# Exponentials in PSUM, V's low part summed by the matmul, a third query/key buffer, and steps with a choice of engine

## Chip, core and metric

The kernel runs on one core of a Trainium2 chip. The metric is device time in microseconds (us); lower is better. Engines: PE (TensorE; PEld is its weight load), DVE (VectorE), ACT (ScalarE), POOL (GpSimd), SP (SyncE, which issues the DMAs).

## What is computed

Block-causal attention over 8 batches of 8 heads, 576 positions, 64 columns per head, and on its output a mixing step of rank 32 over the positions and a feed-forward network (FFN) over the channels:

```python
# per batch and head: S = 576, D = 64, blocks of 64
scores = where(block(i) >= block(j), q @ k.T / sqrt(D), -1e9)
attn = exp(scores - max(scores))
x = (attn / (sum(attn) + 1e-9)) @ v          # heads side by side: 576 x 512
u = x + (x.T @ U @ V).T                      # rank 32
out = u + relu(u @ w_ch1) @ w_ch2            # 512 -> 2048 -> 512
```

All of it is held to float32 accuracy, so a value is split into a high part that the matmul takes (float16, or float32r) and a low part, the difference; a product is then two or three matmuls.

## The kernel before, in words

**Per head.** `split_qk` (L1104) fetches q and k of a head into `raw`. ACT copies them as float32r into `qa` and `ka` (L1117, L1118), POOL subtracts to get the low parts (L1120, L1125), and three DMAs put halves together: `qb` holds q's low part over a copy of its high part, `kb` the reverse for k, where the low part reaches its partitions by a DMA from `raw` (L1136). `qa`, `ka`, `qb`, `kb` and `raw` have `NB` = 2 buffers. `maxima` (L1183) multiplies five row tiles of 128 queries by the keys that they see, DVE takes each row's maximum from PSUM (L1212), PE transposes the maxima (L1219), and DVE spreads them over five rows of `qa` (L1225), so that the next products subtract them. `probabilities` (L1232) forms the transposed scores in three groups of 640, 448 and 512 columns (two matmuls each, L1243 and L1244), ACT takes exponentials from PSUM into `p` in SBUF (L1251), ACT casts `p` to float16 `ph` (L1257), and DVE writes the low part `pl` = `p` - `ph` (L1259). `apply_v` (L1263) runs 15 pairs of matmuls: `ph` times V's high part, a column of ones and V's low part together (129 columns, L1280), and `pl` times V's high part and the ones (65 columns, L1283). The low part's result lies in columns of its own: ACT copies it out (`tmp`, L1292), DVE adds it (`sum`, L1302) and makes the inverse denominators (L1295, L1298), POOL multiplies (`x`, L1307). This runs twice per head, for two and three row tiles.

**Per pair of heads** `split_v` (L1140) scales V by a power of two and splits it; `mix` (L1314) does the rank-32 step. **Per batch** two chunks of 288 positions go through the first half of the FFN (`ffn_chunk`: L631 and L656 on PE, 12 matmuls for each of 8 hidden tiles, whose low part `hl` DVE writes at L639; the chunk's input is split at L600). These matmuls fill PE's waits once a batch's eight heads are done. The FFN's weights are split in `weights_of` (L437; low parts on DVE, L460). After attention the rest of the FFN's first half follows, with more PSUM banks (`bg`), and then its second half as block products (L873).

**Order.** At run time semaphores alone hold the engines to one another; the order of each engine's list is made before: `Plan` (L132) holds tasks with an engine, a planned duration and a priority, plays them through when the program is built, and writes each engine's list in that order. PSUM banks are given out in the same pass, four of one bank (`ba`) and one of two (`bw`). `port` keeps some DVE instructions and POOL's from being planned at one time.

```python
for g, (a, b, tiles) in enumerate(GROUPS):      # L1236
    add("PE", ..., products, [*qa.parts, ka, *qb.parts, *kb.parts], [bank])
    add("ACT", _act(b - a) + 40, pr, exponentials, [bank], [p.parts[g]])
    add("ACT", ..., lambda at=at: nc.scalar.copy(ph[:, at], p[:, at]), ...)
    add("DVE", ..., lambda at=at: nc.vector.tensor_sub(pl[:, at], p[:, at], ph[:, at]), ..., port=True)
```

Of the kernel before, what the change touches and what calls it, by code (L numbers as in the profile page):

```python
# [50 lines left out]
INTO = {"PE": 355, "DVE": 60, "ACT": 60, "POOL": 200, "SP": 60}  # L51
# [14 lines left out]
NB = 2  # L66
# [64 lines left out]

class Plan:  # L132
# [8 lines left out]
    def add(self, engine, ns, prio, fn, reads=(), writes=(), hold=(), after=0, port=False):  # L141

        n = len(self.tasks)
        ns *= 1 + 0.04 * ((n * 40503 + 7919 * VARIANT) % 65536 / 65536 - 0.5)
# [13 lines left out]
        self.tasks.append((engine, ns, prio, fn, deps, after, slots, port or engine == "POOL"))  # L158

    def issue(self, tc):  # L160
        tasks = self.tasks
        users = [[] for _ in tasks]
        left = [len(t[4]) for t in tasks]
        for n, t in enumerate(tasks):
            for d in t[4]:
                users[d].append(n)
        others = [{tasks[u][0] for u in x} for x in users]
        ready = {e: [] for e in ENGINES}
        busy = dict.fromkeys(ready, False)
        port, held, last = False, 0, None  # L170
        behind = mybir.DependencyInfo(mybir.DependencyClass.Sync, mybir.DependencyReason.DATA)
        for n, t in enumerate(tasks):
            if not left[n]:
                heapq.heappush(ready[t[0]], (t[2], n))
# [4 lines left out]
        while done < len(tasks):  # L179
            for e, q in ready.items():  # L180
# [3 lines left out]
                while q:  # L184
                    n = heapq.heappop(q)[1]
                    new = [b for b in tasks[n][6] if b.ap is None]
                    if all(b.pool for b in new) and not (port and tasks[n][7]) and not (e == "POOL" and now < held):
                        break
                    later.append((tasks[n][2], n))
                    n = None  # L190
                else:
                    n = None
# [7 lines left out]
                x = tasks[n][3]()  # L200
# [8 lines left out]
                port = port or tasks[n][7]
                end = now + tasks[n][1]  # L210
                heapq.heappush(events, (end, 0, n))
                t = end + tasks[n][5] + TAIL[e]
                heapq.heappush(events, (t + 35, 1, n))
                for x in others[n]:
                    heapq.heappush(events, (t + INTO[x], 3 + ENGINES.index(x), n))
                if not tasks[n][5]:
                    heapq.heappush(events, (end + (0 if e == "PE" else NEAR), 2, n))
            now = events[0][0]
            while events and events[0][0] <= now:
                _, kind, n, *e = heapq.heappop(events)  # L220
                if e:
                    busy[e[0]] = False
                    continue
                if kind == -1:
                    continue
                if kind == 0:
                    busy[tasks[n][0]] = False
                    port = port and not tasks[n][7]
                    continue
                if kind == 1:  # L230
                    for b in tasks[n][6]:
# [4 lines left out]
                for u in users[n]:  # L236

                    near = tasks[u][0] == tasks[n][0] and not tasks[n][5]
                    if kind == (2 if near else 3 + ENGINES.index(tasks[u][0])):
                        left[u] -= 1  # L240
                        if not left[u]:
                            heapq.heappush(ready[tasks[u][0]], (tasks[u][2], u))
# [21 lines left out]
def attention_then_mixer(  # L264
# [172 lines left out]
    def weights_of(half_bufs, hi, lo, blocks, scale, prio, limit=None):  # L437
# [15 lines left out]
        for n, b in enumerate(half_bufs["out"]):  # L453
            add(
                "ACT", _act(CW, True) + 90, last,
                lambda n=n: nc.scalar.activation(hi(n), raw[:, n, :], AF.Copy, scale=scale[:, 0:1]), [x[n], scale], [b],
            )
            add(
                "DVE", 1.3 * CW, last,
                lambda n=n: nc.vector.scalar_tensor_tensor(  # L460
                    out=lo(n), in0=raw[:, n, :], scalar=scale[:, 0:1], in1=hi(n), op0=ALU.mult, op1=ALU.subtract
                ),
                [x[n], scale, b], [b], port=True,
            )

# [214 lines left out]
    def block_products():  # L680
# [5 lines left out]
        end.writers = [n for n, t in enumerate(plan.tasks) if 0 <= t[2] < 1e6]  # L686
# [328 lines left out]
    raw_r = ring(ap, NB, [P, 2 * S], F32, "raw")  # L1015
    qa_r = [b.split(2) for b in ring(ap, NB, [P, W], F32R, "qa")]
    ka_r = ring(ap, NB, [P, W], F32R, "ka")
    qb_r = [b.split(2) for b in ring(ap, NB, [P, S], F32R, "qb")]
    kb_r = [b.split(2) for b in ring(ap, NB, [P, W], F32R, "kb")]
    p_r = [b.split(3) for b in ring(ap, 2, [P, PW], F32, "p")]  # L1020
    ph_r = [b.split(3) for b in ring(ap, 2, [P, PW + 64], F16, "ph")]
    pl_r = [b.split(3) for b in ring(ap, 2, [P, PW + 64], F16, "pl")]
    mx_r = [b.split(5) for b in ring(ap, 2, [P, P], F32, "mx")]
    vr_r = ring(ap, 2, [P, 10, D], F32, "vr")
# [3 lines left out]
    rv_r = [b.split(2) for b in ring(ap, 2, [P, 5], F32, "rv")]  # L1028
    tmp_r = ring(ap, 2, [P, 3, D], F32, "tmp")
    sum_r = ring(ap, 2, [P, 3, D], F32, "sum")  # L1030
    x_r = [b.split(4) for b in ring(ap, 2, [P, 5, P], F32, "x")]
# [8 lines left out]
    sel = buf(ap, [P, 5, P], F32, "sel")  # L1040
# [3 lines left out]
    marks = p_r[0][low, : 2 * W]  # L1044
    nc.gpsimd.memset(marks, 0.0)
    nc.gpsimd.memset(p_r[0][96:101, W : 2 * W], 1.0)
    for n, fill in enumerate((1.0, NEG)):
        x = marks[:, n * W : (n + 1) * W].rearrange("p (i h c) -> p i h c", i=5, h=2)
# [10 lines left out]
    for n in range(NB):  # L1059
        nc.vector.tensor_copy(qa_r[n][low], marks[:, 0:W])  # L1060
        nc.vector.tensor_copy(ka_r[n][low], marks[:, W : 2 * W])
        nc.vector.memset(f32(qa_r[n][0:64, 0:64]), 0.0)
        nc.vector.memset(f32(ka_r[n][0:64, S:W]), 0.0)
        nc.vector.memset(f32(kb_r[n][:, S:W]), 0.0)
# [403 lines left out]
```

## Time and profile before

| | |
|---|---|
| runs shown | 1183.0, 1181.78, 1183.11 us, median 1183.0 |
| profiled execution | 1183.07 us; its span, first to last instruction, 1181.3 us |
| mean granted TensorE clock | 0.949 of 2.4 GHz |
| busy share of the span | PE 93%, PEld 76%, DVE 84%, ACT 63%, POOL 42% |
| HBM | 76.23 MB read, 29.49 MB written |

How to read it: busy time is the union of an engine's instructions. Back-to-back instructions overlap a little at their ends, so count times mean duration is more than busy time. PE's matmuls overlap, since the pipeline's latency is in each one's duration; their cost is the step from start to start. The granted clock has two levels, 1.2 and 2.4 GHz; a mean between them is a stretch that had both.

### The profile page before, as it was taken

How to read it: one execution, taken by the hardware profiler on the slowest of the kernel's cores; microseconds unless marked ns; L12 is line 12 of the kernel's file. 1: busy time of each engine (PE TensorE's matmuls, PEld its weight loads, DVE VectorE, ACT ScalarE, POOL GpSimd, SP SyncE). 2: the span in 40 equal slices, each digit the busy share in tenths (PEclk: the TensorE clock that was granted, in tenths of full speed). 3: DMA queues.
4: the chain of work that ended last, by engine and by line, in shares of the span. 5: the costliest groups of instructions: out<-in, count | busy, mean ns of one | idle time of the engine just before them, and what ended most of it. 6: DMA issues, size and time to landing. Idle time of an engine off the chain costs nothing.

```text
span 1181.3 us, 25529 instructions
## 1 busy us (share of the span) xinstructions
PE 1095.8 (93%) x9514; PEld 903.3 (76%) x9514; DVE 991.5 (84%) x2120; ACT 747.6 (63%) x1472; POOL 491.6 (42%) x572
## 2 busy tenths in 40 slices
PE   6776897789999999999999999999999999999998
PEld 5665676677888778888888778777777777777777
DVE  7788898989898898888788785264499999999998
ACT  6566786776876887878687775424445455455543
POOL 5654444446757567565665663945400000000000
PEclk7567698979999999999999999999999999999999
DMA  5644555545545554553645432252203412431321
GB/s 135 161 111 138 135 164 161 150 113 169 159 132 151 155 140 123 137 133 92 162 102 155 112 92 61 72 161 63 86 31 111 122 41 82 121 97 40 106 81 41
DMA packets 82924, 135.71 MB, mean 115 GB/s; under 512 B 10352, under 2 KB 54384, under 8 KB 82800
## 3 DMA queue, kind: packets, MB, share of 16 engines
q1 hardware_dynamic: 82800, 134.08, 40.9%
q8 instruction: 75, 1.23, 0.4%
q14 instruction: 49, 0.40, 0.1%
HBM read 76.23 MB, written 29.49 MB: 90 GB/s over the span
## 4 chain that ended last, share of the span: by engine, by line
PE 54%; DVE 22%; ACT 15%; issue 3%; POOL 3%; DMA 2%; SPq 0%; POOLq 0%; ACTq 0%; DVEq 0%
PE bb L873 28%; PE bf L656 6%; DVE mx L1212 5%; DVE pl L1259 4%; PE bf L631 4%; ACT p L1251 4%; ACT ph L1257 3%; PE bg L631 2%; DVE qa L1225 2%; PE bg L656 2%; PE ba L1280 2%; PE ba L1243 1%; DVE hl L639 1%; DVE sum L1302 1%; PE bw L1243 1%
## 5 line engine op out<-in xcount | busy, mean ns | idle before, releaser
L1259 DVE TENSOR_TENSOR pl<-p,ph 128x448 f16<-128x448 f32 (+2 forms) x192 | 141.6, 762 | 10.3 <-ACT ph L1257 9.7
L1280 PE MATMUL ba<-vv,ph 128*128 128x129 f16 x960 | 109.0, 230 | 15.8 <-ACT p L1251 8.1
L656 PE MATMUL bf<-hh,w2h 128*128 128x288 f16 x424 | 121.9, 287 | 0.0
L656 PE MATMUL bf<-hl,w2h 128*128 128x288 f16 x424 | 121.3, 286 | 0.0
L656 PE MATMUL bf<-hh,w2l 128*128 128x288 f16 x424 | 121.3, 286 | 0.0
L631 PEld LDWEIGHTS <-w1h 128*128 128x128 f16 x1024 | 97.3, 99 | 30.0 <-issue 5.4
L656 PEld LDWEIGHTS <-w2h 128*128 128x128 f16 x1024 | 100.6, 98 | 25.5 <-issue 0.7
L873 PE MATMUL bb<-hh,w1h 128*128 128x288 f16 x448 | 118.9, 286 | 0.0
L873 PE MATMUL bb<-hh,w1l 128*128 128x288 f16 x448 | 118.9, 286 | 0.0
L873 PE MATMUL bb<-hh,w2h 128*128 128x288 f16 x448 | 118.9, 286 | 0.0
L873 PE MATMUL bb<-hh,w2l 128*128 128x288 f16 x448 | 118.9, 286 | 0.0
L1257 ACT CAST ph<-p 128x448 f16<-128x448 f32 (+2 forms) x192 | 116.1, 643 | 0.4
L1120 POOL TENSOR_TENSOR qb<-raw,qa 64x576 fp32r<-64x576 f32 x64 | 90.4, 1412 | 49.1 <-DVE pl L1259 14.8
L1283 PE MATMUL ba<-vv,pl 128*128 128x65 f16 x960 | 106.1, 201 | 5.0 <-DVE pl L1259 4.7
L1283 PEld LDWEIGHTS <-pl 128*128 128x128 f16 x960 | 89.9, 102 | 24.2 <-issue 12.2
L801 ACT CAST hh<-hb 128x576 f16<-128x576 f32 x96 | 63.8, 666 | 68.1 <-DVE hb L827 45.8
L873 PEld LDWEIGHTS <-w1h 128*128 128x128 f16 x896 | 87.7, 98 | 22.0
L873 PEld LDWEIGHTS <-w2h 128*128 128x128 f16 x896 | 87.7, 98 | 22.0
L1307 POOL TENSOR_TENSOR x<-sum,rv 128x128 f32<-128x128 f32 (+1 forms) x128 | 57.6, 457 | 105.3 <-DVE sum L1302 54.8
L1280 PEld LDWEIGHTS <-ph 128*128 128x128 f16 x960 | 92.3, 103 | 7.6 <-DVE sum L1302 2.8
L1125 POOL TENSOR_TENSOR raw<-raw,ka 64x576 f32<-64x576 f32 x64 | 90.7, 1417 | 7.8 <-issue 2.1
L873 PE MATMUL bb<-hl,w1h 128*128 128x288 f16 x448 | 91.6, 286 | 0.0
(192 smaller groups left out, 3263.0 us busy)
## 6 DMA issues: line engine op xcount, KB each, us to landing
raw<-in_qk_dram SPq DMA_DIRECT2D x63, 288.0 KB, 3.8
st<-in_w_dram SPq DMA_DIRECT2D x32, 512.0 KB, 3.8
o_d<-ot SPq DMA_DIRECT2D x72, 144.0 KB, 2.3
vr<-in_v_dram SPq DMA_DIRECT2D x32, 320.0 KB, 3.4
qb<-qa SPq DMA_DIRECT2D x64, 144.0 KB, 2.5
kb<-ka SPq DMA_DIRECT2D x64, 144.0 KB, 2.6
kb<-raw SPq DMA_DIRECT2D x64, 144.0 KB, 2.4
ur<-u_d SPq DMA_DIRECT2D x64, 144.0 KB, 2.7
```

What stands on the lines that cost most here:

```text
L631: nc.tensor.matmul(ps[:, :T], w()[wn][:, k, fs], m[k].ap, start=(i == 0), stop=(i == len(ops) - 1))
L656: nc.tensor.matmul(ps[:, :T], w()[wn][:, f, ms], hs[f][x].ap, start=(i == 0), stop=(i == len(ops) - 1))
L801: add("ACT", _act(2 * T, True), E, lambda: nc.scalar.copy(h.ap, x[0]()), [x[1]], [h])
L873: nc.tensor.matmul(bank[:, i, :T], x()[:, w(k)], p.ap[:, k, :], start=first and n == 0, stop=last and n == len(ops) - 1)
L1120: "POOL", 1380, pr, lambda: nc.gpsimd.tensor_sub(qb[top], raw[top, 0:S], f32(qa[top, 64:W])), [raw, qa.parts[0]],
L1125: lambda: nc.gpsimd.tensor_sub(raw[top, S : 2 * S], raw[top, S : 2 * S], f32(ka[top, 0:S])), [ka], [raw],
L1212: lambda i=i, view=view: nc.vector.tensor_reduce(out=mx[:, 96 + i : 97 + i], in_=view(), op=ALU.max, axis=AX.XY if i == 4 else AX.X, negat ...
L1257: add("ACT", _act(b - a, True), pr + 2, lambda at=at: nc.scalar.copy(ph[:, at], p[:, at]), [p.parts[g]], [ph.parts[g]])
L1259: "DVE", _dve(b - a), pr + 2, lambda at=at: nc.vector.tensor_sub(pl[:, at], p[:, at], ph[:, at]),
L1280: nc.tensor.matmul(bank[:, o : o + wide], ph[:, w], vv[:, 5 * s + j, 0:wide], start=(j == 0), stop=False)
L1283: nc.tensor.matmul(bank[:, o : o + D + 1], pl[:, w], vv[:, 5 * s + j, 0 : D + 1], start=False, stop=(j == i))
L1307: lambda: nc.gpsimd.tensor_tensor(out=x[:, cs, 64 * s : 64 * s + 64], in0=total[:, :n, :], in1=rv[:, cs].unsqueeze(2).to_broadcast([P, n, ...
```

## The change

- The exponential writes its result back over the scores in the PSUM bank. The cast to `ph` and the difference `pl` read the bank, which is free only after the difference. `p` is gone; the difference no longer counts as `port`.
- V's low part is multiplied by a matmul of its own (64 columns) that adds onto the high part's columns. All five row tiles share one bank; `tmp` and `sum` are gone, and DVE multiplies by the inverse denominators out of PSUM.
- `qa`, `qb` and the keys, now one tile `kk` for `ka` and `kb`, have three buffers; `raw` keeps two. k's low part is written to its partitions directly, so one of three DMAs per head goes.
- The maxima are copied out of PSUM (`mr`) and spread from there.
- A task may have several engines. Planning gives it to the first free one, unless another would end it sooner, with a handicap in ns as the last number. Such tasks: the casts and differences of q and k, V's scale, cast and difference, the copy and the spreading of maxima, two of `mix`, and the weights' cast and difference.

Short: the parts of the diff that the text speaks of.

```diff
-NB = 2
+NB = 3
...
+                    sooner = any(max(now, until.get(o, 0)) + w[0] + w[3] < now + ns + late for o, w in t.ways.items() if o != e)
+                    if not sooner and all(b.pool for b in new) and not (port and shared) and not (e == "POOL" and now < held):
...
+        add("SP", 550, pr, fetch, writes=[raw], after=DL)
+        for dst, x, b in ((qa[top, 64:W], slice(0, S), qa.parts[0]), (kk[top, 0, 0:S], slice(S, 2 * S), kk.parts[0])):
+            add(
+                "ACT", _act(S, True), pr, lambda dst=dst, x=x: nc.scalar.copy(dst, raw[:, x]), [raw], [b],
+                others=[("DVE", 64 + 0.55 * S, lambda dst=dst, x=x: nc.vector.tensor_copy(dst, raw[:, x]), True, 200)],
+            )
...
+            add(
+                "POOL", 1340, pr, sub(nc.gpsimd), [raw, a], [b], others=[("DVE", 68 + 1.042 * S, sub(nc.vector), True, 600)],
+            )
...
+        add(
+            "ACT", _act(P), pr + 2, lambda: nc.scalar.copy(mr[rows], bank[rows, 0:P]), [bank], [mr],
+            others=[("DVE", _dve(P), lambda: nc.vector.tensor_copy(mr[rows], bank[rows, 0:P]), False, 50)],
+        )
...
+        add(
+            "POOL", 1340, pr + 2, spread(nc.gpsimd), [mr], [qa.parts[1]], others=[("DVE", _dve(W), spread(nc.vector), True, 500)],
+        )
...
             add(
-                "DVE", _dve(b - a), pr + 2, lambda at=at: nc.vector.tensor_sub(pl[:, at], p[:, at], ph[:, at]),
-                [p.parts[g], ph.parts[g]], [pl.parts[g]], port=True,
-            )
+                "ACT", _act(b - a) + 90, pr,
+                lambda view=view: nc.scalar.activation(view(), view(), AF.Exp, bias=lift[:, 0:1], scale=SCALE), [], [bank],
+            )
+            add(
+                "ACT", _act(b - a), pr + 1, lambda at=at, view=view, shaped=shaped: nc.scalar.copy(shaped(ph[:, at]), view()), [bank],
+                [ph.parts[g]],
+            )
+            add(
+                "DVE", _dve(b - a), pr + 1,
+                lambda at=at, view=view, shaped=shaped: nc.vector.tensor_sub(shaped(pl[:, at]), view(), shaped(ph[:, at])),
+                [bank, ph.parts[g]], [pl.parts[g]],
+            )
...
+                        nc.tensor.matmul(bank[:, o : o + D + 1], ph[:, w], vv[:, y, 0 : D + 1], start=(j == 0), stop=False)
+                        nc.tensor.matmul(bank[:, o : o + D], ph[:, w], vv[:, y, D + 1 : 2 * D + 1], start=False, stop=False)
+                        nc.tensor.matmul(bank[:, o : o + D + 1], pl[:, w], vv[:, y, 0 : D + 1], start=False, stop=(j == i))
...
+            lambda: nc.vector.tensor_tensor(
+                out=x[:, :, 64 * s : 64 * s + 64], in0=view()[:, :, 0:D], in1=rv.ap.unsqueeze(2).to_broadcast([P, 5, D]), op=ALU.mult
             ),
```

The planner's table of choices moves the lists as follows (counts of the built programs, whole run): of 128 q/k casts DVE takes 47, of 128 q/k differences 34, of 64 spreads 19 (POOL 45), of 64 copies of maxima 27 (ACT 37), of 32 V casts 11 and differences 5; POOL scales V 14 times of 32. Behind the last matmul of `mix` PE has 888 FFN matmuls of the first half before, and 1,116 now. Ahead of the 16th `hl` on DVE, and of its matmuls on PE:

| count | before | now |
|---|---|---|
| PE: matmuls for maxima / pairs with V / probabilities | 112 / 225 / 204 | 102 / 240 / 200 |
| PE: FFN matmuls, first and second product | 192, 96 | 192, 96 |
| DVE, all | 474 | 435 |
| DVE spreads of maxima; copies `mr` | 18; 0 | 3; 6 |
| DVE row maxima | 93 | 85 |
| DVE low parts of P (`pl`) | 46 | 50 |
| DVE denominators (two instructions each) | 60 | 32 |
| DVE `sum`; scaled write of `x` | 30; 0 | 0; 16 |
| DVE weights: low part; cast | 12; 0 | 6; 2 |
| DVE q/k differences; casts; V casts; `mix` cast; `mix` difference | 0 | 4; 3; 2; 1; 1 |

PE at the start, from the first transpose of maxima (`ba`, `bw` are PSUM banks; `qa_156` and so on are buffers). Before:

```order
L1219 MATMUL ba_92<-ident,mx_170 128x128
L1243 MATMUL bw<-qa_156,ka_158 128x320
L1244 MATMUL bw<-qb_160,kb_162 128x320
L1243 MATMUL bw<-qa_156,ka_158 128x256
L1244 MATMUL bw<-qb_160,kb_162 128x256
```

Now:

```order
L1237 MATMUL ba_92<-ident,mx_169 128x128
L1237 MATMUL ba_93<-ident,mx_170 128x128
L1166 MATMUL ba_92<-ident,vm_179 128x128
L1220 MATMUL bw<-kk_161,qa_158 128x288 x2
L1222 MATMUL bw<-kk_161,qa_158 128x64
L1222 MATMUL ba_95<-kk_161,qa_158 128x448
L1266 MATMUL ba_94<-qa_156,kk_159 128x448
L1267 MATMUL ba_94<-qb_162,kk_159 128x448
```

The third head's maxima now stand ahead of the first head's products.

PE at the first product with V. Before:

```order
L1244 MATMUL ba_95<-qb_161,kb_163 128x192
L1280 LDWEIGHTS ph_166
L1280 MATMUL ba_92<-vv_174,ph_166 128x129
L1283 LDWEIGHTS pl_168
L1283 MATMUL ba_92<-vv_174,pl_168 128x65
```

Now:

```order
L1305 LDWEIGHTS ph_165
L1305 MATMUL ba_93<-vv_176,ph_165 128x65
L1306 LDWEIGHTS ph_165
L1306 MATMUL ba_93<-vv_176,ph_165 128x64
L1307 LDWEIGHTS pl_167
L1307 MATMUL ba_93<-vv_176,pl_167 128x65
```

Each pair became a triple, with a weight load for each matmul.

DVE behind the first head's product with V. Before:

```order
L1295 TENSOR_SCALAR rv_180<-ba_92,sv_178 128x2
L1298 RECIPROCAL rv_180<-rv_180 128x2
L1302 TENSOR_TENSOR sum_185<-ba_92,tmp_183 128x128
L1295 TENSOR_SCALAR rv_180<-ba_94,sv_178 128x3
L1298 RECIPROCAL rv_180<-rv_180 128x3
L1259 TENSOR_TENSOR pl_169<-p_165,ph_167 128x640
L1302 TENSOR_TENSOR sum_184<-ba_94,tmp_182 128x192
```

Now:

```order
L1288 TENSOR_TENSOR pl_168<-ba_92,ph_166 128x512
L1229 TENSOR_REDUCE mx_169<-ba_95 128x1 x2
L1312 TENSOR_SCALAR rv_182<-ba_93,sv_180 128x5
L1315 RECIPROCAL rv_182<-rv_182 128x5
L359 TENSOR_SCALAR z_99<-z_99 96x288
L1320 TENSOR_TENSOR x_184<-ba_93,rv_182 128x5x64
```

Six instructions for a head became three, and the last now writes `x` itself.

## Rows read from the trace of the kernel before

**Rows 1.** The profile's page: busy time of each engine over the span with its share and instruction count, and the span in 40 equal slices (busy tenths; PEclk is the granted TensorE clock in tenths).
```profile
PE 1095.8 (93%) x9514; PEld 903.3 (76%) x9514; DVE 991.5 (84%) x2120; ACT 747.6 (63%) x1472; POOL 491.6 (42%) x572
...
PE   6776897789999999999999999999999999999998
...
PEclk7567698979999999999999999999999999999999
```

**Rows 2.** Busy time by stretch. Columns: stretch, its length, then busy us and instruction count of PE, PEld, DVE, ACT and POOL, the granted clock, the DMA share and GB/s.
```profile
0.00:140.00 140.00, 96.15 (x575) 81.77 (x575) 116.06 (x288) 90.91 (x181) 76.28 (x93) 0.67 0.53 140
140.00:225.00 85.00, 73.92 (x663) 60.93 (x661) 77.70 (x187) 61.05 (x130) 36.47 (x43) 0.93 0.54 152
225.00:300.00 75.00, 64.22 (x591) 53.99 (x590) 67.03 (x174) 56.27 (x115) 38.45 (x51) 0.91 0.49 135
300.00:551.00 251.00, 241.56 (x2355) 204.45 (x2353) 218.75 (x546) 194.93 (x421) 159.17 (x192) 1.00 0.52 140
551.00:737.00 186.00, 179.88 (x1759) 151.98 (x1757) 144.27 (x362) 134.53 (x297) 111.51 (x136) 1.00 0.43 112
737.00:848.00 111.00, 110.06 (x893) 86.73 (x892) 46.68 (x102) 43.01 (x78) 69.74 (x58) 1.00 0.32 97
848.00:1181.30 333.30, 330.05 (x2695) 263.40 (x2692) 321.02 (x466) 166.90 (x254) 0.00 (x0) 1.00 0.26 79
```

**Rows 3.** The chain of waits in order of time (start, us, what), its last long piece.
```profile
848.77 329.29 PE bb L873 x2688
```

**Rows 4.** Timeline, all engines: where the first FFN chunk begins (start, us, engine, line, operation).
```profile
138.57 1.80 DVE L600 SCALAR_TENSOR_TENSOR ul<-ur,sc,uh 128x288 f16<-128x288 f32 x4
...
140.20 1.18 PE L631 MATMUL bf<-uh,w1h 128*128 128x288 f16 x4
```

**Rows 5.** DVE's groups by form in the stretch 0 to 225 us, which ends with the 16th hidden tile of the FFN (L639 x16). Columns: line, engine, operation, out<-in, shapes, count; busy us, mean ns of one; idle time before them and what ended it.
```profile
L1225 DVE TENSOR_TENSOR qa<-ba,sel 5x640 fp32r<-5x640 f32 x18 | 14.9, 830 | 3.1 <-PE ba L1219 2.7
L1212 DVE TENSOR_REDUCE mx<-bw 128x1 f32<-128x576 f32 x19 | 14.3, 751 | 2.0 <-PE bw L1205 1.9
L1259 DVE TENSOR_TENSOR pl<-p,ph 128x640 f16<-128x640 f32 x16 | 13.1, 821 | 2.5 <-ACT ph L1257 2.4
L344 DVE SCALAR_TENSOR_TENSOR z<-st,z 128x512 int32<-128x512 int32 x15 | 12.1, 818 | 0.0
...
L1259 DVE TENSOR_TENSOR pl<-p,ph 128x512 f16<-128x512 f32 x15 | 10.4, 694 | 0.0
L1259 DVE TENSOR_TENSOR pl<-p,ph 128x448 f16<-128x448 f32 x15 | 9.4, 630 | 0.0
...
L1212 DVE TENSOR_REDUCE mx<-ba 128x1 f32<-128x320 f32 x18 | 8.7, 483 | 0.1
...
L639 DVE SCALAR_TENSOR_TENSOR hl<-bf,hh 128x288 f16<-128x288 f32 x16 | 7.2, 452 | 2.0 <-ACT hh L636 1.9
L339 DVE TENSOR_SCALAR z<-z 128x512 int32<-128x512 int32 x15 | 6.4, 439 | 0.0
...
L460 DVE SCALAR_TENSOR_TENSOR w1l<-wr,sc,w1h 128x512 f16<-128x512 f32 x8 | 5.5, 748 | 1.5 <-ACT w1h L456 1.5
L1302 DVE TENSOR_TENSOR sum<-ba,tmp 128x192 f32<-128x192 f32 x15 | 5.1, 338 | 0.0
L1302 DVE TENSOR_TENSOR sum<-ba,tmp 128x128 f32<-128x128 f32 x15 | 4.2, 278 | 0.7 <-ACT tmp L1292 0.5
...
L1295 DVE TENSOR_SCALAR rv<-ba,sv 128x3 f32<-128x3 f32 x15 | 3.3, 218 | 5.4 <-ACT tmp L1292 3.5 <-PE ba L1283 1.8
...
L1298 DVE RECIPROCAL rv<-rv 128x3 f32<-128x3 f32 x15 | 2.7, 178 | 0.5
```

**Rows 6.** Groups by form over the whole span, all engines, same columns as rows 5.
```profile
L1120 POOL TENSOR_TENSOR qb<-raw,qa 64x576 fp32r<-64x576 f32 x64 | 90.4, 1412 | 49.1 <-DVE pl L1259 14.8 <-DVE rv L1295 7.7 <-DVE mx L1212 4.6
...
L1259 DVE TENSOR_TENSOR pl<-p,ph 128x640 f16<-128x640 f32 x64 | 56.9, 889 | 10.0 <-ACT ph L1257 9.4
...
L1251 ACT ACTIVATE p<-bw,lift 128x640 f32<-128x640 f32 x64 | 50.8, 794 | 28.6 <-PE bw L1244 23.2 <-DVE pl L1259 4.9
...
L1257 ACT CAST ph<-p 128x640 f16<-128x640 f32 x64 | 46.7, 730 | 0.1
...
L1321 POOL TENSOR_TENSOR xl<-x,xh 128x512 fp32r<-128x512 f32 x32 | 41.1, 1286 | 21.3 <-DVE pl L1259 7.3 <-ACT xh L1318 6.5 <-DVE wr L352 2.5
...
L827 DVE TENSOR_TENSOR hb<-bb,hb 128x576 f32<-128x576 f32 x32 | 24.2, 755 | 1.4 <-PE bb L873 0.7
L827 DVE TENSOR_TENSOR hb<-hb,hb 128x576 f32<-128x576 f32 x32 | 23.9, 754 | 0.0
```

**Rows 7.** PE's timeline at full clock, the product with V of one head: the first two of its 15 pairs and the last.
```profile
501.28 0.22 PE L1280 MATMUL ba<-vv,ph 128*128 128x129 f16 x1
501.33 0.19 PE L1283 MATMUL ba<-vv,pl 128*128 128x65 f16 x1
501.36 0.22 PE L1280 MATMUL ba<-vv,ph 128*128 128x129 f16 x1
...
502.49 0.22 PE L1280 MATMUL ba<-vv,ph 128*128 128x129 f16 x1
```

**Rows 8.** DMA issues by line: count, KB each, median us from issue to landing.
```profile
kb<-raw SPq DMA_DIRECT2D x64, 144.0 KB, 2.4
```

More of the change, by code (lines that the diff above doesn't have):

```diff
@@ L129, with __init__ @@
 ENGINES = ("DVE", "PE", "ACT", "POOL", "SP")
+class Task:
+    def __init__(self, ways, prio, deps, after, slots):
+        self.ways, self.prio, self.deps, self.after, self.slots = ways, prio, deps, after, slots
+        self.goal, self.near = "any" if len(ways) > 1 else next(iter(ways)), None
 class Plan:
@@ L139, in __init__, with add @@
         self.tasks = []
[L141 removed]
+    def add(self, engine, ns, prio, fn, reads=(), writes=(), hold=(), after=0, port=False, others=()):
         n = len(self.tasks)
[L144 removed]
+        k = 1 + 0.04 * ((n * 40503 + 7919 * VARIANT) % 65536 / 65536 - 0.5)
         deps = set()
@@ L157, in add @@
             b.users += 1
-        self.tasks.append((engine, ns, prio, fn, deps, after, slots, port or engine == "POOL"))
+        ways = {e: (t * k, f, p or e == "POOL", late) for e, t, f, p, late in ((engine, ns, fn, port, 0), *others)}
+        self.tasks.append(Task(ways, prio, deps, after, slots))
     def issue(self, tc):
@@ L185, in issue @@
                     n = heapq.heappop(q)[1]
-                    new = [b for b in tasks[n][6] if b.ap is None]
-                    if all(b.pool for b in new) and not (port and tasks[n][7]) and not (e == "POOL" and now < held):
+                    if taken[n]:
+                        n = None
+                        continue
+                    t = tasks[n]
+                    ns, fn, shared, late = t.ways[e]
+                    new = [b for b in t.slots if b.ap is None]
+                    sooner = any(max(now, until.get(o, 0)) + w[0] + w[3] < now + ns + late for o, w in t.ways.items() if o != e)
+                    if not sooner and all(b.pool for b in new) and not (port and shared) and not (e == "POOL" and now < held):
                         break
-                    later.append((tasks[n][2], n))
+                    later.append((t.prio, n))
                     n = None
@@ L199, in issue @@
                 done += 1
-                x = tasks[n][3]()
+                taken[n] = True
+                t.near = None if t.after else e
+                x = fn()
                 if e == "POOL" and last is not None:
@@ L203, in issue @@
                     last = None
-                if e == "DVE" and tasks[n][7]:
+                if e == "DVE" and shared:
                     last = x
-                    held = now + tasks[n][1] + PORT
+                    held = now + ns + PORT
                     heapq.heappush(events, (held, -1, n))
                 busy[e] = True
[L209 to L217, printed above, removed]
+                port = port or shared
+                end = until[e] = now + ns
+                heapq.heappush(events, (end, 0, n, e, shared))
+                at = end + t.after + TAIL[e]
+                heapq.heappush(events, (at + 35, 1, n))
+                for x in goals[n]:
+                    heapq.heappush(events, (at + INTO[x], 3, n, x))
+                if not t.after:
+                    heapq.heappush(events, (end + (0 if e == "PE" else NEAR), 2, n, e))
             now = events[0][0]
@@ L236, in issue @@
                 for u in users[n]:
-                    near = tasks[u][0] == tasks[n][0] and not tasks[n][5]
-                    if kind == (2 if near else 3 + ENGINES.index(tasks[u][0])):
+                    if tasks[u].goal == e[0] and (kind == 2) == (e[0] == tasks[n].near):
                         left[u] -= 1
                         if not left[u]:
-                            heapq.heappush(ready[tasks[u][0]], (tasks[u][2], u))
+                            arrive(u)
+        self.end = now
 def _act(n, sbuf=False):
@@ L1140, in split_v @@
+        for dst, y, a, b in ((qb[low], qa[top, 64:W], qa.parts[0], qb.parts[1]), (kk[top, 1, 0:S], kk[top, 0, 0:S], kk.parts[0], kk.parts[1])):
+            add("SP", 530, pr, lambda dst=dst, y=y: nc.sync.dma_start(out=f32(dst), in_=f32(y)), [a], [b], after=DL)
     def split_v(p, pr):
```

226 lines of the change are left out of this document (94 added, 132 removed).

## The prediction

> **What bounds the kernel now.** I read the page first: PE is busy for 93% of the span, and its slices show where it is not, the first ten, in which PEclk falls as well [rows 1]. Then the stretches [rows 2]. From 0 to 140 us PE's busy time is 96 of 140 us at a mean granted clock of 0.67, so between the two levels, and most often at 1.2 GHz; DVE is busy for 116. From 140 to 225 us DVE has 78 of 85, its fullest stretch of the attention stage. From 300 us to 737 us, where the last matmul of attention stands, PE is busy for 421 of 437 us at full clock, and DVE for 363. Then comes FFN work alone, and from 848 us a block stage of 2,688 matmuls in 329.3 us, 122.5 ns each [rows 3]; the change touches nothing there. The first FFN chunk could not start before 138.6 us, when its scaled input was split [rows 4]; until then PE has nothing to fill its waits with.
>
> So the time is PE's work plus what PE loses, and it loses most before 225 us, where DVE's list sets the pace: ahead of the 16th hidden tile DVE's 474 instructions keep it busy for 193.8 of 225 us [rows 2, 5]. Two places decide: when the FFN starts to fill PE, and when attention ends with how much FFN work left.
>
> **The start, up to the 16th hidden tile.** The counts stand in the table of the change. PE has issued nearly the same there (192 and 96 FFN matmuls in both; ten fewer matmuls for maxima, 15 more pairs of V). DVE's list differs, each count priced by its row [rows 5]:
> - spreading the maxima: 18 to 3 of 0.830: -12.4 us; six copies of 128 columns in its place, priced by the 128-column sum, 0.278: +1.7.
> - sums of V's two parts: 15 x 0.338 + 15 x 0.278 = 9.2 go; 16 scaled writes of 320 columns come, 0.338 plus twice the 0.060 that 64 columns cost: 0.458, in all 7.3: -1.9.
> - denominators: 60 instructions, about 0.214 and 0.172 (11.6) become 32 on five columns, some 0.436 a head (7.0): -4.6.
> - eight fewer maxima at 0.483, the middle size: -3.9.
> - the low part of P: 46 to 50. It now reads PSUM. The maxima read PSUM too and cost 0.483 at 320 columns and 0.751 at 576, so 0.818 at 640 and 0.707 in the mean of the three sizes, against 0.715 (0.821, 0.694, 0.630): 35.4 against 32.9: +2.5. That PSUM itself costs DVE nothing is in two rows, 755 ns from PSUM and 754 from SBUF for 576 columns [rows 6].
> - low parts of weights: 12 of 0.748 become six differences of about 0.69 and two casts of about 0.44 (priced by L339): -4.0.
> - work that DVE takes over by the planner's choice: four q/k differences of 0.754, three q/k casts of 0.48, two V casts of 0.53, one of each for the mixing (0.44, 0.69): +6.6.
> - one more step each of the four that split a weight block, 0.44 to 0.82: +2.5.
>
> The sum is -13.5, and I take all of it as time, because DVE paces this stretch and PE's own work in it is the same. A cast could cost as much as a difference (0.75), which takes 2 us off; if the waits between engines shrink with the list, as 193.8 of 225 does, it is 16.
>
> **V's low part.** A pair now takes 1.21 us / 14 = 86 ns, 129 columns some 55 and 65 columns some 30, each with its own weight load [rows 7]. The third matmul of 64 or 65 columns should cost what the 65 do: 3 x 30 = 90, so +3.6 ns x 960 pairs, less the 225 pairs ahead of the 16th hidden tile, where PE isn't full: +2.6 us. Bounds: 81 ns if only the columns count, -4 us; three times today's mean of 43 ns, 129, +31 us. I take the first price since its row is the same instruction.
>
> The Trainium skill, TensorE: Matmul & The Clock Gate, section Back-to-back issue gap, speaks against this part: a stream of weight load and matmul pairs sustains some 81 ns per matmul at 128 columns. By it a pair would be 162 ns now and 243 afterwards, 960 x 81 = 78 us more, and the sum 1248; the trace has 86 for two, so the measurement decides.
>
> **What else is moved, and what covers it.** ACT loses 128 copies of V's low part, 47 q/k casts and more, and gains 37 copies of maxima. Its exponentials now write PSUM; no row shows that. The nearest is 0.794 us into SBUF for 640 columns [rows 6]. I take no change, with -0.05 and +0.1 each as ends: 192 x 0.1 = 19 us on an engine idle for 107 of 437 us from 300 to 737 [rows 2], so at nothing. If that cover were gone, the cast behind it and P's low part would be late. The Trainium skill, ScalarE: Activation LUTs, section Step-by-step: what each stage is for, calls PSUM the lower-latency destination; no run here shows it yet, and by it this term could only fall.
>
> A PSUM bank is now held until DVE has taken P's low part. The widest bank serves 1,920 columns of maxima and products (0.9 us at 30 ns for 65 [rows 7]), two reductions (1.0 [rows 5]), exponential 0.8, cast 0.7, difference 0.8: 4.2 us, some 5.5 with the hops, where a head comes every 11.5 (737 us / 64). So it is covered, but PE's maxima for the next head queue behind it. Spreading on POOL waits for a copy on ACT or DVE and takes longer than DVE's 0.83; POOL's nearest row, 1.286 for 512 columns, gives 1.5 for 640. That is 1 us more in a head's chain, 45 times; with a third buffer another head's products lie beside it, and without them 17 early heads would cost up to 17 us. Against it stand V's shorter end (one write where there were a copy, a sum and a POOL product) and 64 DMAs of 2.4 us that no longer stand between a difference and its products [rows 8], each one issue less on SP. I set these against each other at nothing. POOL loses 128 products and some differences.
>
> **The sum.** The profiled execution took 1183.07 us, 0.07 above the median of the runs: 1183.1 - 13.5 + 2.6 = 1172.2; I say 1172.
>
> **The other account, and the rivals.** In the new order attention ends with 1,116 FFN matmuls to go, not 888. That is 228 x 122.5 ns = 27.9 us more behind it, so attention must end 27.9 + 2.6 us sooner, at 707 us, to break even, and at 695 for my number. By the prices above DVE's list to the end of attention changes by: spreads -37.4, copies +7.6, sums -10.1, denominators -21.5, P's low part -11 (0.889 over the run to 0.818, and so for the others [rows 5, 6]), weights -4.6, work taken over +68, fewer FFN tiles -7: -16. So DVE's 623.8 busy us [rows 2] become 608, and 695 means that DVE is 87.5% busy.
>
> - **DVE paces all of attention (slower, 0.26).** DVE keeps its share over the stage, 623.8 / 737 = 85%: attention ends at 718, and the time is 1183 + 27.9 + 2.6 - 19 = 1195. The point that decides is a share of 86%. For it: the work that DVE takes over eats most of its savings. Against it: the share was 87% up to 551 us and fell to 78% after, where PE was 97% busy and DVE waited for PE.
> - **Choice closes DVE's gaps (0.20).** With two engines for a step and P's low part out of POOL's way (14.8 us of POOL's idle time ahead of L1120 ended with L1259, and that instruction grew from 0.821 early to 0.889 overall [rows 5, 6]) DVE reaches 90%: attention ends at 675, and 1183 + 27.9 + 2.6 - 61 = 1152. The Trainium skill, SBUF — State Buffer, section Who interferes with whom, says that a DVE instruction with two SBUF inputs contends with GpSimd's reads and one with at most one doesn't; by it P's 192 differences leave the contest and some 115 casts and differences of DVE enter it.
> - **The early gain is given back (0.08).** The FFN starts sooner but waits for batch 1's heads as before: 1183, no change.
> - **V is bound by its loads (0.03).** At 129 ns a pair, where PE is full, the end moves by +31 - 13.5: 1201.
>
> **How the numbers follow.** My forecast, 1160 to 1180 us by the two ends named for the start and V's lower bounds, has 0.43. The range reaches to both larger rivals with 2 or 3 us for their shares: 1149 to 1196; V's loads and the far ends of those two stay outside. A change under 0.2%, 2.4 us, can't be told from none. Faster: 0.43 + 0.20 = 0.63; same 0.08; slower 0.26 + 0.03 = 0.29.
>
> **What would show it.** The 16th hidden tile near 212 us; the first split of FFN input near 125; attention's last matmul at about 695 with DVE 87% busy up to there; V's three steps about 30 ns each at full clock; the exponentials within 0.1 us of their old times; PE over 95% busy from 300 us on. I am wrong if attention ends after 707, if PE's products wait for banks by more than 0.3 us a head, or if V's triple takes over 110 ns.

## The result, and the profile after

The changed kernel takes 1142.9 us (median of four runs, 1140.5 to 1144.0) against 1183.05 (1181.8 to 1185.2) for the kernel before: ratio 0.966, 95% interval 0.9635 to 0.9677, 40 us faster. The forecast was 1172, 11 us faster.

The page: PE's share rose from 93 to 95%, DVE's from 84 to 86%, ACT's and POOL's fell [rows 1]. PE's low slices end earlier.

```profile
PE 1081.7 (95%) x10474; PEld 894.8 (78%) x10474; DVE 986.0 (86%) x2025; ACT 683.9 (60%) x1315; POOL 463.6 (41%) x461
...
PE   5767888899999999999999999999999999999998
...
PEclk6778898799999999999999999999999999999999
```

Stretches, in the columns of [rows 2]: up to the first FFN matmul (120.2 us; 140.2 before [rows 4]), up to the 16th hidden tile's low part (201.6; before 225), the full-clock middle, the whole of attention, and what follows.

```profile
0.00:120.20 120.20, 84.56 (x760) 72.46 (x761) 105.28 (x256) 82.58 (x165) 80.50 (x82) 0.75 0.51 139
0.00:201.60 201.60, 157.00 (x1495) 131.44 (x1496) 182.45 (x435) 143.68 (x291) 128.34 (x126) 0.83 0.56 153
300.00:551.00 251.00, 246.70 (x2846) 210.67 (x2845) 241.28 (x573) 180.54 (x380) 146.20 (x147) 1.00 0.47 128
0.00:670.70 670.70, 614.13 (x6664) 522.41 (x6665) 611.83 (x1444) 467.66 (x969) 389.27 (x395) 0.94 0.48 131
670.70:809.00 138.30, 138.30 (x1126) 109.56 (x1125) 53.95 (x118) 49.23 (x94) 74.30 (x66) 1.00 0.30 87
809.00:1141.60 332.60, 329.31 (x2689) 262.81 (x2686) 320.27 (x465) 167.03 (x254) 0.00 (x0) 1.00 0.26 79
```

Attention's last matmul of `mix` stands at 670.3 us instead of 737, with DVE busy for 91% up to there. The chain's last long piece begins 39.7 us earlier and is as long as before [rows 3], so the whole gain lies ahead of it:

```profile
809.03 329.29 PE bb L892 x2688
```

Groups by form, in the columns of [rows 5] and [rows 6]:

```profile
L1246 POOL TENSOR_TENSOR qa<-mr,sel 5x640 fp32r<-5x640 f32 x45 | 69.8, 1553 | 34.1 <-ACT mr L1241 8.1 <-DVE qa L1246 6.6 <-DVE vm L1158 4.3
L1142 POOL TENSOR_TENSOR qb<-raw,qa 64x576 fp32r<-64x576 f32 x48 | 69.1, 1439 | 51.8 <-ACT qa L1135 8.8 <-PE bf L675 6.6 <-issue 5.7
...
L1288 DVE TENSOR_TENSOR pl<-bw,ph 128x640 f16<-128x640 f32 x64 | 52.1, 813 | 6.5 <-ACT ph L1283 6.1
L1280 ACT ACTIVATE bw<-bw,lift 128x640 f32<-128x640 f32 x64 | 49.2, 768 | 43.0 <-PE bw L1267 39.9 <-DVE z L359 1.5 <-DVE rv L1315 1.0
...
L1283 ACT CAST ph<-bw 128x640 f16<-128x640 f32 x64 | 44.7, 699 | 0.8 <-PE ba L1307 0.4
...
L1320 DVE TENSOR_TENSOR x<-ba,rv 128x320 f32<-128x320 f32 x64 | 30.9, 484 | 0.5
...
L1312 DVE TENSOR_SCALAR rv<-ba,sv 128x5 f32<-128x5 f32 x64 | 13.9, 217 | 11.8 <-PE ba L1307 11.6
L1142 DVE TENSOR_TENSOR qb<-raw,qa 64x576 fp32r<-64x576 f32 x16 | 13.4, 835 | 0.0
L1315 DVE RECIPROCAL rv<-rv 128x5 f32<-128x5 f32 x64 | 12.2, 191 | 2.2
```

V's triples at full clock, the first and the twelfth of a run on PE:

```profile
500.08 0.19 PE L1305 MATMUL ba<-vv,ph 128*128 128x65 f16 x1
500.11 0.20 PE L1306 MATMUL ba<-vv,ph 128*128 128x64 f16 x1
500.14 0.19 PE L1307 MATMUL ba<-vv,pl 128*128 128x65 f16 x1
...
501.09 0.19 PE L1305 MATMUL ba<-vv,ph 128*128 128x65 f16 x1
```

Eleven steps in 1.01 us: 92 ns a triple, 31 ns a matmul.

### The profile page after: what moved, and what is told of

Its sections match the earlier page's. It is cut to its first block, busy times and chain, and to the rows that moved or that the text cites. A ratio compares the mean times of both kernels' runs of the same rounds, so it can differ in the third digit from the quotient of the medians.

```text
span 1141.6 us, 27034 instructions
## 1 busy us (share of the span) xinstructions
PE 1081.7 (95%) x10474; PEld 894.8 (78%) x10474; DVE 986.0 (86%) x2025; ACT 683.9 (60%) x1315; POOL 463.6 (41%) x461
## 4 chain that ended last, share of the span: by engine, by line
PE 67%; DVE 21%; ACT 4%; issue 3%; DMA 2%; POOL 2%; SPq 0%; DVEq 0%; POOLq 0%; ACTq 0%
PE bb L892 29%; PE bf L675 8%; PE bf L650 8%; DVE mx L1229 5%; PE bg L675 4%; DVE pl L1288 4%; PE bg L650 3%; PE ba L1305 2%; PE ba L1306 2%; PE ba L1307 2%; PE ba L1266 1%; PE bw L1266 1%; PE bw L1267 1%; DVE hl L658 1%; PE ba L1267 1%
## 5 line engine op out<-in xcount | busy, mean ns | idle before, releaser
L675 PE MATMUL bf<-hh,w2h 128*128 128x288 f16 x384 | 110.6, 288 | 1.4 <-DVE hl L658 1.4
L675 PE MATMUL bf<-hh,w2l 128*128 128x288 f16 x384 | 109.9, 286 | 0.0
L675 PE MATMUL bf<-hl,w2h 128*128 128x288 f16 x384 | 109.8, 286 | 0.0
L1305 PE MATMUL ba<-vv,ph 128*128 128x65 f16 x960 | 108.4, 199 | 0.9 <-DVE pl L1288 0.6
L1306 PE MATMUL ba<-vv,ph 128*128 128x64 f16 x960 | 107.6, 200 | 0.0
L1305 PEld LDWEIGHTS <-ph 128*128 128x128 f16 x960 | 92.7, 100 | 5.3 <-issue 3.0
L1306 PEld LDWEIGHTS <-ph 128*128 128x128 f16 x960 | 93.5, 101 | 1.9 <-issue 1.0
L1307 PEld LDWEIGHTS <-pl 128*128 128x128 f16 x960 | 93.6, 103 | 0.1
L892 PE MATMUL bb<-hl,w2h 128*128 128x288 f16 x448 | 91.5, 286 | 0.0
L1280 ACT ACTIVATE ba<-ba,lift 128x448 f32<-128x448 f32 (+1 forms) x128 | 79.0, 630 | 19.2 <-PE ba L1267 18.8
L1142 POOL TENSOR_TENSOR qb<-raw,qa 64x576 fp32r<-64x576 f32 x48 | 69.1, 1439 | 51.8 <-ACT qa L1135 8.8
```

Source lines behind the costliest of these rows:

```text
L675: nc.tensor.matmul(ps[:, :T], w()[wn][:, f, ms], hs[f][x].ap, start=(i == 0), stop=(i == len(ops) - 1))
L892: nc.tensor.matmul(bank[:, i, :T], x()[:, w(k)], p.ap[:, k, :], start=first and n == 0, stop=last and n == len(ops) - 1)
L1142: sub = lambda e, dst=dst, x=x, y=y: lambda: e.tensor_sub(dst, raw[:, x], f32(y))
L1280: lambda view=view: nc.scalar.activation(view(), view(), AF.Exp, bias=lift[:, 0:1], scale=SCALE), [], [bank],
L1305: nc.tensor.matmul(bank[:, o : o + D + 1], ph[:, w], vv[:, y, 0 : D + 1], start=(j == 0), stop=False)
L1306: nc.tensor.matmul(bank[:, o : o + D], ph[:, w], vv[:, y, D + 1 : 2 * D + 1], start=False, stop=False)
```

## One account for all runs

PE's work is nearly the same in all these kernels, so they are compared by **PE's loss**: a stretch less its matmuls, each priced by its columns at full clock (288 take 122.5 ns [rows 3], others in proportion; floors of 29 ns, and of 58 or 110 for narrow float32 ones, estimates from the shortest steps in the traces). Time at half clock counts as loss. The level of a loss hangs on these floors; its differences between runs move by 1 or 2 us with other floors. Stretches: to the first FFN matmul ("start"), to 250 us, to attention's last matmul of `mix`, and the block stage. The time is the median of a kernel's runs; the losses are those of its profiled execution.

| run | us | first FFN | start | to 250 | to end | block | end of attention |
|---|---|---|---|---|---|---|---|
| before | 1183 | 140 | 88 | 36 | 37 | 0 | 737 |
| before, other orders (e7, e8) | 1179, 1180 | 135, 138 | 84, 85 | 35, 36 | 39, 36 | 0 | 718, 733 |
| changed | 1143 | 120 | 68 | 31 | 21 | 0 | 670 |
| changed, other orders (e5, e6) | 1158, 1149 | 127, 120 | 71, 70 | 39, 29 | 24, 26 | 0 | 658, 644 |
| changed, fixed engines (e1) | 1165 | 129 | 80 | 34 | 28 | 0 | 696 |
| changed, two buffers (e2) | 1199 | 123 | 74 | 30 | 25 | 45 | 759 |
| changed, exponentials in SBUF (e3) | 1179 | 125 | 75 | 43 | 37 | 0 | 659 |
| changed, V's old form (e4) | 1175 | 125 | 68 | 40 | 44 | 0 | 666 |
| before + exponentials in PSUM (e9) | 1161 | 121 | 72 | 34 | 32 | 0 | 702 |
| the same, `pl` kept as `port` (e16) | 1171 | 142 | 89 | 30 | 25 | 6 | 743 |
| before + V in PSUM (e10) | 1155 | 131 | 79 | 33 | 20 | 3 | 718 |
| the same + DVE load (e14) | 1159 | 127 | 77 | 36 | 19 | 3 | 720 |
| the same + ACT load (e15) | 1148 | 130 | 77 | 25 | 22 | 0 | 704 |
| the same, two banks (e17) | 1162 | 133 | 82 | 29 | 29 | 0 | 698 |
| before + third buffer (e11) | 1191 | 130 | 77 | 44 | 45 | 0 | 663 |
| choice of engine, no PSUM part (e12) | 1202 | 137 | 88 | 39 | 54 | 0 | 746 |
| before + both PSUM parts (e13) | 1147 | 125 | 76 | 26 | 23 | 0 | 712 |
| the same, other order (e18) | 1148 | 117 | 68 | 32 | 25 | 0 | 691 |

The end of attention doesn't follow the time: what PE doesn't do of the FFN before it, it does behind it. Place by place, the change took 20 us from the start, 4 up to 250 us, 16 from there to attention's end and 1 behind it; V's added matmuls give back 2 at these prices.

## Experiments

**One part undone.** Four runs, each from the changed kernel.

e1, every step on the engine that it had before:
```diff
-... for e, t, f, p, late in ((engine, ns, fn, port, 0), *others)}
+... for e, t, f, p, late in ((engine, ns, fn, port, 0),)}
...
-add("POOL", 1340, pr + 2, spread(nc.gpsimd), [mr], [qa.parts[1]], others=[("DVE", ...)])
+add("DVE", _dve(W), pr + 2, spread(nc.vector), [mr], [qa.parts[1]], port=True)
```
(V's scale to ACT and the weights' difference to DVE likewise. DVE's spread has the `port` mark here, which it had not in the kernel before.)

> The changed kernel with one engine for every step, the one that it had before (maxima spread on DVE, weights' difference on DVE, V scaled on ACT, q and k cast on ACT and subtracted on POOL); everything else as changed. Theory C (the choice of engine closes DVE's gaps): most of the 40 us go, 1170 us or more, attention's last matmul of mixing at 700 us or later instead of 670.7, DVE's share up to it back to 85 to 87% from 91%. Theory P (the exponential in PSUM shortens what ACT hands to DVE) and theory V (V's sum in PSUM): within 8 us of 1143, and DVE's share stays at 90% or more. Theory B (third query/key buffer): the same, within 8 us.

e2:
```diff
-NB = 3
+NB = 2
```


> The changed kernel with two query/key buffers instead of three. Theory B: 1165 us or more, and PE's waits for casts of k and for the spread maxima (21 us before, hardly any in the changed kernel) come back. Theories C, P and V: within 8 us of 1143.

e3:
```diff
-nc.scalar.activation(view(), view(), AF.Exp, ...), [], [bank]
+nc.scalar.activation(shaped(p[:, at]), view(), AF.Exp, ...), [bank], [p.parts[g]]
...
+nc.vector.tensor_sub(pl[:, at], p[:, at], ph[:, at]), ..., port=True
```


> The changed kernel with the exponentials written to SBUF, cast and split from there, and the difference planned as sharing a port with POOL, as before; the other parts as changed. Theory P: 1160 us or more, the difference of 640 columns back at 0.85 us or more, POOL's idle time ahead of its q/k differences longer, DVE's share under 89%. Theories C, B and V: within 8 us of 1143.

e4:
```diff
-apply_v(h, pr + 30)
+for g in (1, 0): apply_v(h, g, pr + 30)   # tmp, sum and POOL's product as before
```


> The changed kernel with V's low part in columns of its own, as before: copied out by ACT, added by DVE, multiplied by POOL, in two rounds of denominators per head. Theory V: 1160 us or more, DVE's idle time ahead of denominators and sums back near 15 us (it was 14.6 us before the copies on ACT). By DVE's list alone, sums and denominators that come back (10 + 21 us) less the scaled writes (64 x 0.48 = 31 us, gone): about equal, so theories C, B and P: within 8 us of 1143.

Measured: 1165.1 (0.985, 0.982 to 0.988), 1199.1 (1.014, 1.011 to 1.017), 1179.3 (0.996, 0.994 to 0.998) and 1174.6 (0.994, 0.992 to 0.996), ratios to the kernel before. Each undone part loses 22 to 56 us, in all 146 where the whole change gained 40: no theory alone, and no sum. e1 fell between the two times that were expected of it; in e3 DVE was busy for 91% of attention, where under 89% was expected. Without choice the start loses 12 us of the 22. With two buffers PE's loss in attention is nearly as small as with three; the 45 us lie in the block stage, whose first weights are prepared once attention is done. Attention ended at 759 us with 468 FFN matmuls to go, and PE stood. PE's longest waits between 800 and 900 us of that run (line waited for, us, times, longest):

```profile
PE bb L892 <- ACT w2h L756: 23.2, 2, 17.7
...
PE bb L892 <- POOL w2l L757: 4.5, 2, 2.7
PE bb L892 <- ACT st L850: 4.3, 2, 3.9
```

The granted clock was 0.81 in these 100 us, and 1.00 in the kernel before. In the changed kernel 1,116 matmuls cover that work. Theories P and V are borne out in size: with either part undone the loss from 250 us to attention's end is again 37 to 44.

**Another order of the same work.** Only the number changed that seeds the small spread on planned durations.
```diff
-VARIANT = 12
+VARIANT = 5      # e6, e8: 23
```


> The changed kernel with another seed (5 for 12) of the small spread, up to 2% either way, that planning puts on each step's duration: the same work, another order. If the order that planning happened to find carries much of the 40 us, or of the 22 to 56 us that undoing one part lost: 1155 us or more. If the parts carry them: within 6 us of 1143.

> The same with seed 23. Order theory: 1155 us or more. Parts: within 6 us of 1143.

> The kernel before with seed 5. Order theory: over 10 us away from 1183. Parts: within 6 us of 1183.

> The kernel before with seed 23. Order theory: over 10 us away from 1183. Parts: within 6 us of 1183.

Measured: 1158.2 (0.980, 0.977 to 0.983) and 1148.7 (0.972, 0.969 to 0.975); 1179.4 (0.998, 0.996 to 1.000) and 1179.5 (0.998, 0.996 to 1.000). Three orders of the changed kernel spread over 15 us with mean 1150, three of the kernel before over 4 with mean 1181. So the change is worth some 31 us; its own order gave 7 more, and that of the kernel before 2. The 7 are luck. A difference of under 15 us between two kernels, each in one order, shows nothing about a part.

**One part alone.** From the kernel before.

e9 takes the three tasks of `probabilities` as the diff above has them, e10 `apply_v`, e11 this:
```diff
-NB = 2
+NB = 3
```
e12 is the changed kernel with the edits of e2, e3 and e4 together.

> The kernel before with the exponential written back to PSUM and split from there, alone. If the parts add up, each is worth here what its removal cost from the changed kernel (36 us): 1147. If they hang together (a bank that is held longer needs V's one bank per head; without it PE waits for banks): no gain, 1175 or more, and PE's loss between 250 us and the end of attention, 37 us in the kernel before, stays there or grows to some 44, as in the run with V's old form.

> The kernel before with V's low part summed in PSUM and scaled by one DVE write, alone. Adding up: 1183 - 32 = 1151. Hanging together: 1170 to 1183, PE's loss behind 250 us near 37 still (as in the run with exponentials in SBUF).

> The kernel before with three query/key buffers, alone. In the changed kernel the third buffer was worth 10 us up to the block stage (6 of them ahead of the first FFN matmul) and 45 us in it, where the weights' second half came late. Adding up: some 10 us faster, 1173, as the kernel before has 888 FFN matmuls to cover those weights and loses nothing there. If DVE's list alone paces the start: within 4 us of 1183.

> The changed kernel with exponentials in SBUF, V's old form and two query/key buffers: what is left is the choice of engines, the maxima's copy and k's low part written in place. Choice theory for the start: the first FFN matmul some 10 us sooner than before (130 instead of 140), the loss behind 250 us as before (37), 1165 to 1175. If choice needs the other parts: 1180 or more.

Measured: 1161.2 (0.983, 0.981 to 0.985), 1154.7 (0.978, 0.976 to 0.980), 1190.8 (1.009, 1.006 to 1.011), 1201.9 (1.018, 1.016 to 1.019). The two PSUM parts each gain alone, 20 and 27 us: V's is what adding up gave (1151) within 4 us, that of the exponentials lies between the two expectations. The third buffer alone gains nothing: it is 9 us slower, less than an order can move. The choice without the PSUM parts loses 21 us, the second of its two expectations (1180 or more); what it loses them by is open.

**Both PSUM parts, and what each works by.** e13 has the edits of e9 and e10. Its order again: e18. The others, from e10 and e9:
```diff
 # e14, behind the write of x
+add("DVE", 495, pr, lambda: nc.vector.tensor_reduce(out=idle[:, 0:1], in_=zero.ap.unsqueeze(1).to_broadcast([P, 3, P]), op=ALU.max, axis=AX.XY), [rv], [idle])
 # e15
+for n in (128, 192): add("ACT", _act(n), pr, ... nc.scalar.copy(idle[:, :, 0 : n // 2], zero...), [rv], [idle])
 # e16
-                [bank, ph.parts[g]], [pl.parts[g]],
+                [bank, ph.parts[g]], [pl.parts[g]], port=True,
 # e17
+tiles = ((0, 1), (2, 3, 4))[g]   # a bank, denominators and a write of x for each
```


> The kernel before with both PSUM parts: exponentials written back to PSUM and split from there, and V's low part summed in PSUM with one scaled write. No choice of engine, two query/key buffers. If the two add up: 1181 - 20 - 27 = 1134, under the changed kernel. If they overlap (both take the same waits of PE away): 1145 to 1155, no better than V's part alone by more than the 10 us that another order moves.

> The kernel of e10 (V's part alone, 1154.7) with one more DVE instruction per head behind the inverse denominators, a maximum over 384 columns of zeros that nobody reads, about 0.5 us: what V's part took off DVE's list (89.1 us before, 57.4 after, over 64 heads). If DVE's shorter list is the gain: 1172 or more, and PE's loss behind 250 us back from 20 us to 30 or more. If it is the chain or the bank: within 8 us of 1155.

> The kernel of e10 with two more ACT copies per head of 128 and 192 columns that nobody reads: what V's part took off ACT (37.6 us over the run). If ACT's shorter list is the gain: 1172 or more. If DVE's list, the chain or the bank is: within 8 us of 1155.

> The kernel of e9 (exponentials in PSUM alone, 1161) with the difference pl planned as sharing the port with POOL, as before; the instructions are the same, only the order differs. If the planner's freedom to set pl beside POOL is the gain: 1173 or more. If it is the shorter exponentials and casts or the source in PSUM itself: within 8 us of 1161.

> The kernel before with V's low part summed in PSUM and x written by DVE out of PSUM, but in two rounds per head with a bank each, as before. If the shorter way from V's last matmul to x is the gain: within 8 us of 1155, PE's loss from 250 us to the end of attention 18 to 24 us. If the one bank is: 1170 or more, and that loss 30 or more. By DVE's list it has four instructions of denominators and two writes per head, about 0.35 us more than e10, which e14 showed to be worth 5 us at most.

> The kernel of e13 (both PSUM parts, no choice, two buffers) with seed 5. If the two parts are the whole change and the rest is order: between 1140 and 1160, where the three orders of the changed kernel lie (1143, 1149, 1158). If e13 was a lucky order and the choice and the third buffer carry 10 us or more: 1160 or more.

Measured: e13 1147.0 (0.969, 0.967 to 0.972), e14 1159.5 (0.981, 0.979 to 0.983), e15 1148.2 (0.971, 0.969 to 0.972), e16 1170.8 (0.990, 0.988 to 0.992), e17 1162.4 (0.982, 0.980 to 0.983), e18 1148.1 (0.970, 0.969 to 0.971).

*The whole.* e13 and e18, with no choice and two buffers, take 1147 and 1148, where three orders of the changed kernel take 1143 to 1158. Alone they gained 20 and 27, together 36, so they overlap, as the second expectation of e13 had it. The two PSUM parts are the change; choice, third buffer and the copied maxima add nothing that stands out from the orders. None of these kernels beats the changed one in its own order.

*V.* e14 put 64 instructions back on DVE, 34.8 us, and lost 5, as little as an order can move; PE's loss behind 250 us stayed at 19:

```profile
L1298 DVE TENSOR_REDUCE idle<-zero x64: 530/543/545, 26.1 to 710.7; 128x1 f32<-128x384 f32 x64
```

e15 put ACT's copies back and lost nothing. So V's gain isn't DVE's or ACT's shorter list. The way from V's last matmul to the written `x` (worked out from starts and ends in the traces) went from about 3.7 us in the mean to 1.85 (e10). e17 keeps that (1.82) with two banks: the loss is 29, between 20 (e10) and 37 (before), and the time 1162, 8 over e10. So most of the gain needs no single bank; the bank may carry the other 8 us, which orders alone can move, so that share stays open. One rival no run has tested: V's part also takes 128 products off POOL, 58.5 us busy with 105.2 us of idle time ahead of them, and POOL's other steps stand behind them in its list. A shorter way and a freer POOL aren't told apart. The kernel before:

```profile
L1307 POOL TENSOR_TENSOR x<-sum,rv 128x192 f32<-128x192 f32 x64 | 33.0, 515 | 59.7 <-DVE sum L1302 40.2 <-DVE z L344 8.3 <-DVE pl L1259 6.3
...
L1307 POOL TENSOR_TENSOR x<-sum,rv 128x128 f32<-128x128 f32 x64 | 25.5, 398 | 45.5 <-DVE sum L1302 14.6 <-DVE pl L1259 12.5 <-DVE z L344 5.7
```

*Exponentials.* What POOL waited for, whole run of the kernel before, its three largest entries ending with P's low part:

```profile
POOL x L1307 <- DVE pl L1259: 18.8, 11, 5.4
POOL qb L1120 <- DVE pl L1259: 14.8, 6, 4.1
...
POOL t L1340 <- DVE pl L1259: 13.8, 7, 3.7
```

All such entries sum to 90.7 us over 49 waits. In e9 they are 3.3, the changed kernel has none, and e16, which differs from e9 by one `port` mark, has 88.8. The mark isn't planning alone: `Plan.issue` makes POOL's next instruction depend on the marked DVE instruction, which the chip waits for. In e9 the entry of L1120 is gone, and POOL waits there for ACT's cast:

```profile
POOL qb L1120 <- ACT qa L1117: 63.0, 33, 4.9
```

With the mark back (e16):

```profile
POOL x L1313 <- DVE pl L1265: 21.0, 15, 3.7
```

The first FFN matmul is then at 142 us instead of 121, more than orders moved it (5 to 8 us), the start's loss 89 instead of 72, and the time 1171, 10 us more, 6 of them in the block stage. That falls between e16's two expectations and within what orders move. Nor did POOL wait less there: its idle time ahead of L1120 is 71.7 us in e9 and 69.3 in e16, with other releasers, and e3, which has the mark too, has its first FFN matmul at 125. So it is shown that the mark makes POOL wait for `pl`, but not how much of the part's 20 us that is worth. The exponentials' and casts' own durations and the source in PSUM are the rest, not told apart.

## Why the prediction missed

- **What is moved, set at nothing: the step that failed.** I priced V's shorter end and the exponentials in PSUM only by busy time of the lists, and put the rest "against each other at nothing". Alone they gain 27 and 20 us, together 36 (e13). The rows had a sign of it: POOL's 14.8 us ended by `pl` stood in [rows 6], and I used it in a rival only; of the other 76 us of POOL's waits on `pl`, by `x`, `t` and others, I priced none. And I described `port` as planning, not as a wait. Which of these waits carries the 36 us stays open.
- **Nothing behind 225 us.** PE's loss from 250 us to attention's end, 37 us, fell to 21 (24 and 26 in the other orders). I left it unpriced: that is 11 to 16 us of the miss, and mostly V's (20 in e10).
- **The start.** DVE's list up to the 16th hidden tile was to shrink to 193.8 - 13.5 = 180.3 us; 182.5 is measured. The prices were right. But the tile came 23 us earlier, not 13.5: DVE was 90% busy, not 86%. Against the mean of before's three orders (121 us) the loss up to 250 us is 22 less in two orders of the changed kernel and 11 in the third, so part of this is the order.
- **DVE paces.** It doesn't. e13 has DVE busy for 583.5 of 711.9 us, 82%, and takes 1147; e14 adds 35 us to its list and loses 5. The forecast list of 608 us came out at 611.8, right and beside the point. e13 up to attention's last matmul, in the columns of [rows 2]:

```profile
0.00:711.88 711.88, 656.53 (x6961) 557.91 (x6962) 583.54 (x1366) 502.41 (x1018) 369.54 (x393) 0.95 0.52 139
```

- **The other account.** Attention's end as the mark of time fails: at 659 us it goes with 1179 (e3), at 712 with 1147 (e13). The arithmetic with 1,116 matmuls left was right, but the end itself had no bound from DVE's share.
- **Choice closes DVE's gaps, 1152.** Nearest in number, with attention ending at 675 (670 measured) and DVE at 90% (91%). Its cause fell: without choice the same time stands (e13, e18), so its number is luck. Where the third buffer and the copied maxima are in, fixing the engines does cost 22 us (e1), 15 against the mean of the three orders: choice may pay back what those cost, which isn't shown.
- **V's triple** was put at 90 ns; 92 is measured, which makes that term 4 us, not 2.6. An estimate by the 81 ns per matmul at 128 columns of the Trainium skill, TensorE: Matmul & The Clock Gate, section Back-to-back issue gap, made it 243; the trace speaks against it and agrees with the old rows.
- **Exponentials** came 26 ns cheaper at 640 columns (768 against 794), inside the ends I named, and P's low part 813 where I said 818. The Trainium skill, ScalarE: Activation LUTs, section Step-by-step: what each stage is for, calls PSUM the lower-latency destination, and the trace agrees by these 26 ns.
- **Banks.** PE's waits for `bw` that ended with `pl` are 15.3 us over the run, 0.24 a head, and those of the products alone (L1266, for `bw` and `ba`, ended by `pl` or `x`) some 12: under the 0.3 I named. All of attention's matmuls together, for both kinds of bank, wait 21.4 us for `pl` and `x`, 0.33. The largest waits of PE now:

```profile
PE bw L1266 <- DVE pl L1288: 8.2, 9, 1.8
PE bw L1220 <- DVE pl L1288: 7.1, 7, 2.3
```

None of the three signs that I named for being wrong came: attention ended at 670, before 707, the products waited under 0.3 us a head for banks, and the triple took under 110 ns. All three looked for a slower kernel, and the miss was on the other side.

## What to carry to other kernels

Price a removed instruction by who waits for it, on every engine, before its busy time; look for waits that the code itself adds between engines too. Where two streams share an engine, follow that engine's loss by stretches; the end of one stream moves with the order and is no measure. Where an order is made by a planner, run two or three more orders of both kernels first: here they moved the changed kernel by 15 us with no change in work.

## What the chip showed that was not expected

An exponential back into its PSUM bank and the cast out of PSUM were 26 and 31 ns cheaper at 640 columns than by way of SBUF (768 and 699 against 794 and 730). The difference `pl` with one source in PSUM no longer slows down late in the run: 813 in the mean, where the SBUF form went from 821 early to 889 overall. DVE's q and k differences, with both sources in SBUF, took 835 and 890 where 754 was assumed from a row of the same width, and the spreading 899 on DVE where it was 830 early in the kernel before, with its source in PSUM:

```profile
L1246 DVE TENSOR_TENSOR qa<-mr,sel 5x640 fp32r<-5x640 f32 x19 | 17.1, 899 | 0.6
...
L1142 DVE TENSOR_TENSOR kk<-raw,kk 64x576 fp32r<-64x576 f32 x18 | 16.0, 890 | 0.6
```

The traces show what goes with it, when these instructions are sorted by whether a POOL instruction ran at the same time. Of the 34 q and k differences 12 overlapped one and took 1078 ns in the mean; the 22 others took 747, what was assumed. Of the 64 `pl` of 640 columns in the kernel before, both sources in SBUF, 20 overlapped one and took 1045, the 44 others 818. With one source in PSUM it made no difference: 815 for 55 `pl` of the changed kernel that overlapped, 804 for 9 that didn't. POOL's ends in a profile are rough, and no run here takes POOL away.
